# Loads of the first batch and the last two groups in a top-k attention + highway kernel

## The chip, the cores and the metric

One core of one Trainium2 chip. The time is the device time of the kernel in microseconds; the kernel before was run three times and the median is given. Beside it stands one profiled execution, whose span runs from its first to its last instruction.

## What is computed

For 8 batches of 8 heads, with 576 rows of 64 numbers: scores are q·kᵀ/8; in each row of scores only the 32 largest are kept; softmax over these; the product with v. The heads are laid side by side into a matrix x of 4608 x 512, and a highway layer follows.

```python
scores = scale * np.matmul(q, k.transpose(0, 1, 3, 2))
kth = np.partition(scores, -top_k, axis=-1)[..., -top_k:-top_k + 1]
scores = np.where(scores >= kth, scores, -1000000000.0)
attn = np.exp(scores - max); attn = attn / (sum + 1e-09)
x = heads_side_by_side(np.matmul(attn, v))
H = np.maximum(x @ w_h, 0.0)
T = 1.0 / (1.0 + np.exp(-(x @ w_t + b_t)))
out = T * H + (1.0 - T) * x
```

## The kernel before

**Units.** The rows of a batch are taken as five query tiles: four of 128 rows and a rest of 64 rows, in which two heads share the 128 partitions. A *group* is a query tile with all 8 heads of a batch; the two rests of two neighbouring batches are joined into one highway group. Inside a group the work goes in *pairs* of tiles (two tiles of 128 x 576 scores), and two pairs are a *quad*. `n` counts the pairs, 144 in all. `step` runs over them, and each step works on several pairs at different stages.

**A pair.** `scores` (L190) makes 8 matmuls into `ps`, a PSUM tile of four banks of which there is one (`bigps`). `evac` (L210): ScalarE writes relu(scores) to a buffer `z`. `tree` (L221): VectorE takes the maximum of the two halves of each row into `hi`; this reads `ps`, and frees it. For a quad `folds` (L236) halves twice more (`hh`, `h3`) and puts minima into the list buffer `w2`. `minima` (L251): GpSimd forms the matching minima of `hh` and `hi` by integer arithmetic, in four instructions. `tops` and `rest` (L272, L293) are VectorE's lists: MAX8 and MATCH_REPLACE8 on these short rows until the 32nd largest of each row stands in `m4`. `mask` (L368): ScalarE makes a penalty `pen` from z and that threshold. `trans` (L411): TensorE transposes z and adds the penalty into PSUM, 4 chunks per tile into `zt` (two buffers) and the last chunk of both tiles into `zr` (one buffer); ScalarE takes exp of each into `et`. `av` (L444): product with v into the rest of `zr`; ScalarE copies it to `xs`.

**A group.** `norm` (L478) divides by the sums, which gives `g.x`. The highway layer is `ffn_x` (transposes of x to `xT`, and half of x as `xh`), `ffn_h` (x·w_h), `ffn_r`/`ffn_d` (relu, minus xh), `ffn_t` (x·w_t, Tanh), `ffn_e` and `ffn_o` (products and sum, and the DMA of the result). Its PSUM comes from `ffn_bank` (L492).

**Order.** Nearly all instructions of TensorE, VectorE, ScalarE and GpSimd go through `Pinned` (L25): they keep the order in which the program writes them on their engine. So the profile gives L35, the line of that helper, for nearly all of them, and tiles tell them apart. DMAs by `nc.sync` (the SP queue) and by the plain `nc.scalar` are not pinned; a scheduler places them.

**The start.** `early` (L726) prepares the first batch: for each of four head pairs `prep_pair` (L130) loads k and q (each as two halves of 128 KB and a rest of 32 KB), transposes them by TensorE (`kqps`), and copies them to `kT` and `qT`, q by VectorE. Load buffers are in pairs (`ldpool`, 2). For pair 0 the second halves of k and q go by ScalarE's queue, unpinned; all others by SP. 24 warm-up transposes of the identity stand before the first real ones.

**The end.** From L855 the last three pairs (`m`, `m+1`, `m+2`) and the last two groups (`gp`, the second-last; `gl`, the last, `final`) are written out by hand. `judge_lists`, `judge_scales` and `judge` reduce flags over the whole run, which tell whether a slow exact loop has to be run after all (L893); it is not run with this data.

Of the kernel before, what the change touches and what calls it, by code (L numbers as in the profile page):

```python
# [8 lines left out]
AF = mybir.ActivationFunctionType  # L9
# [30 lines left out]
class PinnedCore:  # L40
    def __init__(self, tc):
        for name in ("tensor", "vector", "scalar", "gpsimd"):
            setattr(self, name, Pinned(tc, getattr(tc.nc, name)))
        self.sync = tc.nc.sync


class Group:
# [19 lines left out]
class Ops:  # L67


    def __init__(self, ctx, tc, shared, exact):  # L70
        self.tc = tc
        self.nc = tc.nc if exact else PinnedCore(tc)
        self.__dict__.update(shared)
        self.exact = exact
        s = "g" if exact else ""

        def pool(name, bufs, **kw):
            return ctx.enter_context(tc.tile_pool(name=name + s, bufs=bufs, **kw))

        PS = bass.MemoryType.PSUM  # L80
        self.ldpool = pool("ld", 2)
        self.kqpool = pool("kq", 1 if exact else 2)
        self.scpool = pool("sc", 2) if exact else None
        self.treepool = pool("tree", 3)
        self.wpool = pool("w", 4)
        self.lpool = pool("l", 2)
        self.etpool = pool("et", 2)
        self.xpool = pool("x", 2)
        self.fpool = pool("f", 2)
        self.bigps = pool("bigps", 1, space=PS)  # L90
        self.ztps = pool("ztps", 2, space=PS)
        self.zrps = pool("zrps", 1, space=PS)
        self.fps = pool("fps", 1, space=PS)
        self.st = {}
        self.quads = {}

    def load_pair(self, src, hp, name, eng=None, other=None):
        nc, D, S, R, P = self.nc, self.D, self.S, self.R, self.P  # L100
        JP = J * P
        eng = eng or nc.sync
        if name == "vin":
            t = self.ldpool.tile([P, 2, J + 1, D], FP32, tag=name, name=name)
            eng.dma_start(
                t[:, :, 0:J, :].rearrange("p h j d -> p h (j d)"),
                src(hp, 0, JP).rearrange("h (p j) d -> p h (j d)", j=J),
            )
            eng.dma_start(t[0:R, :, J, :], src(hp, JP, S).rearrange("h p d -> p h d"))
            return t  # L110
        t = self.ldpool.tile([P, J + 1, 2, D], FP32, tag=name, name=name)
        for hh in range(2):
            (other if other and hh else eng).dma_start(
                t[:, 0:J, hh, :],
                src(hp, 0, JP)[hh].rearrange("(p j) d -> p j d", j=J),
            )
        rest = lambda: eng.dma_start(
            t[0:R, J, :, :], src(hp, JP, S).rearrange("h p d -> p h d")
        )
        if other:  # L120
            return t, rest
        rest()
        return t
# [6 lines left out]
    def prep_pair(self, srcs, hp, prep, qeng=None, early=False):  # L130
# [2 lines left out]
        JP = J * P  # L133
        kT, qT, vb = prep
        ins = {}

        def load():
            if qeng:
                ins["k"], k_rest = self.load_pair(srcs[1], hp, "kin", None, qeng)
                ins["q"], q_rest = self.load_pair(srcs[0], hp, "qin", None, qeng)  # L140
                k_rest()
                q_rest()
            else:
                ins["k"] = self.load_pair(srcs[1], hp, "kin")
                ins["q"] = self.load_pair(srcs[0], hp, "qin")
            if not early:
                load_v()

        def load_v():
            ins["v"] = self.load_pair(srcs[2], hp, "vin")  # L150

        def main(name, dst):
            if early:
                kqps = self.ztps.tile([P, 512], FP32, tag="zt", name="kqps")
            else:
                kqps = self.fps.tile([P, 512], FP32, tag="fp", name="kqps")
            for c in range(J):
                nc.tensor.transpose(
                    kqps[:, c * P : (c + 1) * P],
                    ins[name][:, c, :, :].rearrange("p h d -> p (h d)"),  # L160
                    self.ident[:],
                )
            if early and name == "q":
                nc.vector.tensor_copy(dst[:, hp, 0:JP], kqps[:])
            else:
                nc.scalar.copy(dst[:, hp, 0:JP], kqps[:])
# [69 lines left out]
    def folds(self, k, g, pi):  # L236
# [4 lines left out]
        if pi == 0:  # L241
# [2 lines left out]
        vec.tensor_tensor(hh[:], hi[:, :, 0:H2], hi[:, :, H2:H1], ALU.max)  # L244
        a, b = hh[:, :, 0:H3], hh[:, :, H3:H2]
        vec.tensor_tensor(h3[:], a, b, ALU.max)
        return vec.tensor_tensor(
            g.w2[:, 2 * pi : 2 * pi + 4, H3:H2], a, b, ALU.min
        )

    def minima(self, k, after):  # L251

# [3 lines left out]
        hi, hh, h3 = self.quads[k]  # L256
        z = self.zbufs[k % NZ]
        sci, hii, hhi = [a[:].bitcast(I32) for a in (z, hi, hh)]
        head = gp.tensor_tensor(hhi, hii[:, :, 0:H2], hhi, ALU.subtract)
        self.tc.add_manual_dep(  # L260
            head.ins,
            after.ins.name,
# [2 lines left out]
            ),  # L265
            reason="after the folds",
        )
        gp.tensor_tensor(hhi, hhi, hii[:, :, H2:H1], ALU.add)
        gp.tensor_tensor(hii, sci[:, :, 0:H1], hii, ALU.subtract)
        gp.tensor_tensor(hii, hii, sci[:, :, H1:S], ALU.add)  # L270

    def tops(self, g, t, h3, hl):  # L272
# [135 lines left out]
                dst, pen[:, ti, cs], self.nident[:], start=False, stop=True  # L408
            )

    def trans(self, n, final=False):  # L411
        nc, P = self.nc, self.P
        JP = J * P
        z, pen = self.st[n].pop("z"), self.st[n].pop("pen")
        et = self.etpool.tile([P, 2, J + 1, P], BF16, tag="et", name="et")

        def ends():
            zr = self.zrps.tile([P, 512], FP32, tag="zr", name="zr")
            for ti in range(2):
                self.chunk_T(zr[:, ti * P : (ti + 1) * P], z, pen, ti, J)  # L420
            nc.scalar.activation(
# [4 lines left out]
            )  # L426
            self.st[n].update(et=et, zr=zr)

        if not final:
            ends()  # L430
        for ti in range(2):
            zt = self.ztps.tile([P, JP], FP32, tag="zt", name="zt")
            for c in range(J):
                self.chunk_T(zt[:, c * P : (c + 1) * P], z, pen, ti, c)
# [3 lines left out]
                AF.Exp,  # L438
                scale=self.scale,
            )  # L440
        if final:
            ends()

    def av(self, n, g, pi, vb):  # L444
        nc, P = self.nc, self.P
# [32 lines left out]
    def norm(self, g):  # L478
# [3 lines left out]
        rinv = self.scales[:, g.gi, :]  # L482
        nc.vector.reciprocal(rinv[0:ql, :], xs3[:, :, D])
        g.x = self.xpool.tile([P, H * D], FP32, tag="x", name="x")
        (nc.vector if g.final else nc.gpsimd).tensor_tensor(
            g.x[0:ql, :].rearrange("p (h d) -> p h d", h=H),
            xs3[:, :, 0:D],
            rinv[0:ql, :].unsqueeze(2).to_broadcast([ql, H, D]),
            ALU.mult,
        )  # L490

    def ffn_bank(self, g, name, other=False):  # L492
        if g.final or other:
            return self.ztps.tile([self.P, 512], FP32, tag="zt", name=name)
        return self.fps.tile([self.P, 512], FP32, tag="fp", name=name)
# [87 lines left out]
    def ffn_o(self, g, *dsts):  # L583
        ql = g.rows
        o = self.fpool.tile([self.P, self.dm], FP32, tag="o", name="o")
        eng = self.nc.vector if g.final else self.nc.gpsimd
        eng.tensor_tensor(o[0:ql, :], g.x[0:ql, :], g.d[0:ql, :], ALU.add)
        n = ql // len(dsts)
        for i, dst in enumerate(dsts):
            self.nc.sync.dma_start(dst, o[i * n : (i + 1) * n, :])  # L590
# [3 lines left out]
def kernel(  # L594
# [65 lines left out]
    with ExitStack() as cm:  # L660
# [62 lines left out]
        def have(n):  # L723
            return 0 <= n < NPR

        early = [  # L726
            prep(0, hp, nc.scalar if hp == 0 else None, True) for hp in range(NHP)
        ]
        early[0][0]()
        early[1][0]()  # L730
        warm = ops.fps.tile([P, 512], FP32, tag="fp", name="warm")
        for _ in range(24):
            ops.nc.tensor.transpose(warm[:, 0:P], ident[:], ident[:])
        for piece in early[0][1:4]:
            piece()
        ops.scores(0, *pairs[0], preps[0])
        ops.evac(0)
        ffn = []
# [16 lines left out]
            vec.tensor_reduce(bad[:, 3:4], bad[:, 0:3], op=ALU.max, axis=AX.X)  # L755

        def judge():
            bps = ops.fps.tile([P, 512], FP32, tag="fp", name="bps")
            ops.nc.tensor.transpose(bps[0:1, 0:P], bad[:, 3:4], ident[:])
            vec.tensor_reduce(flag_f[:], bps[0:1, 0:P], op=ALU.max, axis=AX.X)  # L760
            vec.tensor_copy(flag[:], flag_f[:])
# [11 lines left out]
        while step <= NPR:  # L773
            n = step
            if have(n):
# [3 lines left out]
                if n + 1 < NHP:  # L779
                    for piece in early[n + 1][1:4]:  # L780
                        piece()
                    if n + 2 < NHP:
                        early[n + 2][0]()
                    else:
                        for e in early[0:2]:
                            e[5]()
            if n == 5:
                load_weights()
# [24 lines left out]
            if NHP - 1 <= n < 2 * NHP - 1:  # L813
                e = n + 1 - NHP
                early[e][4]()
                if e + 2 < NHP:
                    early[e + 2][5]()
            ended = False
            if have(n - 5):
                g, pi = pairs[n - 5]  # L820
# [1 line left out]
            if n % 2:  # L822
                gens = ops.lists_rest(n // 2 - 1, *pairs[n - 3]) if have(n - 3) else []
                late = gens[2:]
                gens = gens[0:2]
                ops.run(gens)
                if kind == "t":
                    ops.ffn_e(fg)
# [1 line left out]
                ops.run(late, 2)  # L830
            else:
                ops.run(late)
                gens = ops.lists(n - 2, *pairs[n - 2]) if have(n - 2) else []
                ops.run(gens, 2)
                if kind == "h":
                    ops.ffn_d(fg)
                if ended:
# [26 lines left out]
        ops.ffn_e(fg)  # L864
        ops.ffn_o(fg, *out_rows(fg))
        ops.run(late)
        values(m)
        ops.trans(m + 1)
        ops.norm(gp)
        ops.settle(gl)  # L870
        ops.mask(m + 2, *pairs[m + 2])
        ops.ffn_x(gp)
        values(m + 1)
        ops.trans(m + 2, final=True)
        ops.ffn_h(gp)
        ops.ffn_r(gp)
        ops.ffn_d(gp)
        values(m + 2)
        ops.norm(gl)
        ops.ffn_t(gp)  # L880
        ops.ffn_x(gl)
        ops.ffn_e(gp)
        ops.ffn_o(gp, *out_rows(gp))
        judge_lists()
        judge_scales()
        ops.ffn_h(gl)
        ops.ffn_r(gl)
        ops.ffn_d(gl, ops.ffn_t(gl))
        judge()
        ops.ffn_e(gl)  # L890
        ops.ffn_o(gl, *out_rows(gl))

    taken = nc.values_load(flag[0:1, 0:1], min_val=0, max_val=1)  # L893
    with tc.If(taken > 0):
# [64 lines left out]
```

## Time and profile before

| what | us |
|---|---|
| median of three runs | 888.23 (886.67 to 888.36) |
| the profiled execution | 888.35 |
| its span | 886.6 |
| first scores start on TensorE | 8.41 |
| VectorE's last list ends | 863.6 |
| VectorE's last instruction ends | 879.36 |
| mean granted TensorE clock | 0.95 |

A view by stretches gives VectorE 0.03 us of work in the first 7.6 us, 5.40 in the next 13.4, 814.18 in the 819 us from 21 to 840, 23.13 in the 23.6 to 863.6, and 8.61 in the last 15.8 before 879.4. In timeline lines the first column is the start in us from the span's start, the second the time from the first start to the last end of the merged instructions, then engine (ACTq, SPq: the queue that issues a DMA), line, operation, tile written <- tiles read, shapes, count, and in brackets the idle time before it and what ended it. In lines of waits, the numbers are us in total, times, and the longest.

### The profile page before, as it was taken

To read this page: it belongs to the slowest core of one execution; us is meant where nothing else is said; L and a number is where in the kernel's file an instruction comes from. 1 tells how busy PE (TensorE), PEld (TensorE's weight loads), DVE (VectorE), ACT (ScalarE), POOL (GpSimd) and SP (SyncE) were. 2 spreads that over 40 slices of the span, in tenths; PEclk is the share of its full clock that TensorE was granted. 3 is DMA by queue.
4 is the path that set the end of the run, shared out by engine and by line. 5 is a ranking of instruction groups with operands and counts; after the bars stand their busy time and mean duration, and the time that the engine had idled before them with its cause. 6 is when DMAs were issued, how large, how long until landed. Compare 5 with 4: busy or idle time off the path is not lost.

```text
span 886.6 us, 20024 instructions
## 1 busy us (share of the span) xinstructions
PE 712.9 (80%) x6573; PEld 503.8 (57%) x6573; DVE 851.3 (96%) x4198; ACT 700.7 (79%) x1333; POOL 724.8 (82%) x452
## 2 busy tenths in 40 slices
PE   6678978878877888788788797887988789877874
PEld 5456655655555565565565565665555556555553
DVE  2999999999999999999999999999999999999993
ACT  3688878888788887888788887888978888777762
POOL 5788888888878889888887888878887888888872
PEclk9799999999999999999999999999999999898888
DMA  6362110322012220212202211032201300000001
GB/s 150 78 115 74 44 36 13 81 54 53 14 39 67 54 53 13 54 41 53 54 13 65 60 45 42 14 81 65 53 14 28 80 13 14 13 13 1 14 25 28
DMA packets 96671, 40.29 MB, mean 45 GB/s; under 512 B 82608, under 2 KB 91952, under 8 KB 96560
## 3 DMA queue, kind: packets, MB, share of 16 engines
q1 hardware_dynamic: 94304, 37.51, 16.5%
q0 software_dynamic: 1200, 1.18, 0.8%
q8 instruction: 53, 0.87, 0.4%
q14 instruction: 58, 0.48, 0.2%
q10 hardware_dynamic: 1056, 0.26, 0.1%
HBM read 30.67 MB, written 9.44 MB: 45 GB/s over the span
## 4 chain that ended last, share of the span: by engine, by line
DVE 86%; PE 6%; ACT 5%; issue 1%; POOL 0%; ACTq 0%; POOLq 0%
DVE w L35 45%; DVE m L35 17%; DVE hi L35 10%; DVE hh L35 6%; DVE h L35 3%; PE ps L35 3%; DVE d L35 3%; ACT z L35 2%; ACT et L35 2%; PE zt L35 1%; ACT pen L35 1%; PE zr L35 1%; PE tps L35 1%; PE warm L35 1%; DVE scales L35 0%
## 5 line engine op out<-in xcount | busy, mean ns | idle before, releaser
L35 PE MATMUL ps<-kT,qT 64*128 64x64 f32 (+3 forms) x1280 | 215.4, 462 | 91.1 <-DVE hi L35 86.5
L35 ACT ACTIVATE z<-ps 128x1152 f32<-128x1152 f32 x144 | 163.2, 1133 | 111.0 <-PE ps L35 109.5
L35 ACT ACTIVATE pen<-z,m 128x576 bf16<-128x576 f32 x288 | 225.9, 786 | 0.1
L35 PE MATMUL zt<-ident,z 128*128 128x128 f32 x1152 | 225.5, 289 | 0.3
L35 PEld LDWEIGHTS ps<-kT,qT 64*128 64x128 f32 (+1 forms) x1280 | 108.2, 184 | 191.2 <-DVE hi L35 95.8
L35 PE MATMUL zt<-nident,pen 128*128 128x128 bf16 x1152 | 214.7, 225 | 0.0
L35 POOL TENSOR_TENSOR hh<-hi,hh 128x576 int32<-128x576 int32 x72 | 101.7, 1413 | 124.3 <-DVE w L35 124.3
L35 POOL TENSOR_TENSOR hi<-hi,z 128x1152 int32<-128x1152 int32 x72 | 190.3, 2642 | 5.6
L35 POOL TENSOR_TENSOR hi<-z,hi 128x1152 int32<-128x1152 int32 x72 | 189.3, 2629 | 5.6
L35 PEld LDWEIGHTS zt<-ident,z 128*128 128x128 f32 x1152 | 169.7, 147 | 19.3 <-ACT xT L35 1.0
L35 ACT ACTIVATE et<-zt 128x512 bf16<-128x512 f32 x288 | 161.6, 606 | 13.5 <-PE zt L35 12.6
L35 PEld LDWEIGHTS <-pen 128*128 128x128 bf16 x1440 | 160.0, 111 | 1.5 <-ACT pen L35 1.3
L35 DVE MAX8 m<-w 128x8 f32<-128x168 f32 x576 | 160.3, 320 | 0.0
L35 DVE MAX8 w<-hi 128x8 f32<-128x288 f32 x288 | 116.7, 447 | 0.1
L35 DVE TENSOR_TENSOR hi<-ps,z 128x576 f32<-128x576 f32 x144 | 106.5, 740 | 8.2 <-ACT z L35 8.2
L35 POOL TENSOR_TENSOR hh<-hh,hi 128x576 int32<-128x576 int32 x72 | 101.3, 1407 | 5.6
L35 PE MATMUL zr<-v,et 128*128 128x65 bf16 (+1 forms) x1600 | 89.6, 196 | 15.9 <-ACT et L35 13.0
L35 PEld LDWEIGHTS <-et 128*128 128x128 bf16 (+1 forms) x1600 | 70.3, 101 | 52.6 <-ACT et L35 36.5
L35 DVE MATCH_REPLACE8 w<-m,w 128x168 f32<-128x168 f32 x288 | 89.3, 318 | 0.0
L35 DVE MAX8 w<-hh 128x8 f32<-128x72 f32 x576 | 84.1, 219 | 0.0
L35 PE MATMUL zr<-ident,z 128*128 128x128 f32 x288 | 74.9, 314 | 3.6 <-ACT xs L35 3.5
L35 DVE TENSOR_TENSOR hh<-hi 128x576 f32<-128x576 f32 x72 | 62.2, 865 | 2.5
(71 smaller groups left out, 1153.9 us busy)
## 6 DMA issues: line engine op xcount, KB each, us to landing
vin<-in_v_dram SPq DMA_DIRECT2D x32, 256.0 KB, 3.0
out_dram<-o SPq DMA_DIRECT2D x32, 256.0 KB, 2.3
kin<-in_k_dram SPq DMA_DIRECT2D x63, 128.0 KB, 3.0
qin<-in_q_dram SPq DMA_DIRECT2D x63, 128.0 KB, 2.9
kin<-in_k_dram SPq DMA_DIRECT2D x32, 32.0 KB, 2.5
qin<-in_q_dram SPq DMA_DIRECT2D x32, 32.0 KB, 2.5
vin<-in_v_dram SPq DMA_DIRECT2D x32, 32.0 KB, 2.6
out_dram<-o SPq DMA_DIRECT2D x8, 128.0 KB, 2.4
```

The source lines that it names most:

```text
L35: return self._tc.keep_in_program_order(fn(*args, **kw))
```

## The change

At the start: the loads of the first batch are pinned to their queues (a new `queue` wraps `nc.sync`, and `ops.nc.scalar` takes the place of `nc.scalar`); there are three load buffers, so the loads of three head pairs are written first; the second halves of k and q go by ScalarE's queue for head pairs 0 and 1; v follows behind the loads of the fourth pair. The 24 warm-ups become 12 before k's transposes and 3 before q's. The q copies of head pairs 2 and 3 go to ScalarE. For the first quad VectorE makes the minimum of `hh` itself, so that GpSimd has two instructions there, not four, and the first two rounds of its lists are written into step 1.

```diff
-        self.ldpool = pool("ld", 2)
+        self.ldpool = pool("ld", 2 if exact else 3)
...
+        eng = nc.queue if early else nc.sync
...
-            if qeng:
-                ins["k"], k_rest = self.load_pair(srcs[1], hp, "kin", None, qeng)
-                ins["q"], q_rest = self.load_pair(srcs[0], hp, "qin", None, qeng)
+            if early:
+                ins["k"], k_rest = self.load_pair(
+                    srcs[1], hp, "kin", eng, qeng, True
+                )
+                ins["q"], q_rest = self.load_pair(
+                    srcs[0], hp, "qin", eng, qeng, True
+                )
                 k_rest()
                 q_rest()
...
-            if early and name == "q":
+            if early and name == "q" and hp < 2:
                 nc.vector.tensor_copy(dst[:, hp, 0:JP], kqps[:])
...
+        if k == 0:
+            last = vec.tensor_tensor(
+                hh[:], hi[:, :, 0:H2], hi[:, :, H2:H1], ALU.min
+            )
+        return last
...
-        early[0][0]()
-        early[1][0]()
+        for e in early[0:3]:
+            e[0]()
...
-        for _ in range(24):
-            ops.nc.tensor.transpose(warm[:, 0:P], ident[:], ident[:])
-        for piece in early[0][1:4]:
-            piece()
+        spin(12)
+        early[0][1]()
+        spin(3)
+        early[0][2]()
+        early[0][3]()
...
+                if n == 1:
+                    opening = ops.lists(0, *pairs[0])
+                    ops.run(opening, 2)
```

At the end: `trans` is split into `parts`, so that the transposes, exps and penalties of the last pairs can be written in another order. The four banks of `ps`, no longer needed for scores, are handed out: three to the second-last group's highway layer, the fourth to the last pair in place of `zr`, and two of the first again to the last group's Tanh product. The last group's x, xT and final product are done in halves of 256 columns, each half of the result leaving on SP's and ScalarE's queues at once (64 rows each). The flag reductions move to earlier places on VectorE, and `norm` of the second-last group moves from GpSimd to VectorE.

```diff
+    def final_t(self, g, banks):
+        nc, n_g = self.nc, self.n_g
+        W = self.dm // 2
+        g.tp = [b[:, 0:W] for b in banks]
+        for j, tp in enumerate(g.tp):
+            cs = slice(j * W, (j + 1) * W)
+            for i in range(n_g):
+                nc.tensor.matmul(
+                    tp, g.xT[:, i, :], self.wt[:, i, cs],
+                    start=(i == 0), stop=False,
+                )
+            nc.tensor.matmul(
+                tp, self.cst[:], self.bt[:, cs], start=False, stop=True
+            )
+            nc.scalar.activation(tp, tp, AF.Tanh)
+    def final_o(self, g, dsts, queues):
+        vec, P = self.nc.vector, self.P
+        W = self.dm // 2
+        n = P // len(dsts)
+        o = self.fpool.tile([P, self.dm], FP32, tag="o", name="o")
+        for j, tp in enumerate(g.tp):
+            cs = slice(j * W, (j + 1) * W)
+            vec.scalar_tensor_tensor(
+                out=g.d[:, cs], in0=tp, scalar=1.0, in1=g.d[:, cs],
+                op0=ALU.add, op1=ALU.mult,
+            )
+            vec.tensor_tensor(o[:, cs], g.x[:, cs], g.d[:, cs], ALU.add)
+            for i, dst in enumerate(dsts):
+                queues[i].dma_start(dst[:, cs], o[i * n : (i + 1) * n, cs])
...
     def ffn_bank(self, g, name, other=False):
+        if g.last and not g.final:
+            return self.spare.pop(0)
...
         values(m)
-        ops.trans(m + 1)
+        part, ends = ops.parts(m + 1)
+        part(0)
+        ops.mask(m + 2, *pairs[m + 2], tis=(0,))
+        part(1)
+        ops.mask(m + 2, *pairs[m + 2], tis=(1,))
+        ends()
         ops.norm(gp)
         ops.settle(gl)
-        ops.mask(m + 2, *pairs[m + 2])
-        ops.ffn_x(gp)
+        part, ends = ops.parts(m + 2, banks[3])
+        ends()
+        part(0)
         values(m + 1)
-        ops.trans(m + 2, final=True)
-        ops.ffn_h(gp)
-        ops.ffn_r(gp)
-        ops.ffn_d(gp)
+        ops.ffn_x(gp)
+        part(1)
+        judge_lists()
         values(m + 2)
         ops.norm(gl)
-        ops.ffn_t(gp)
-        ops.ffn_x(gl)
+        ops.ffn_h(gp)
+        ops.ffn_r(gp)
+        ops.final_x(gl)
+        ops.ffn_d(gp)
+        ops.ffn_t(gp)
+        judge_scales()
         ops.ffn_e(gp)
         ops.ffn_o(gp, *out_rows(gp))
-        judge_lists()
-        judge_scales()
         ops.ffn_h(gl)
         ops.ffn_r(gl)
-        ops.ffn_d(gl, ops.ffn_t(gl))
+        ops.ffn_d(gl)
         judge()
-        ops.ffn_e(gl)
-        ops.ffn_o(gl, *out_rows(gl))
+        ops.final_t(gl, banks[0:2])
+        ops.final_o(gl, out_rows(gl), (nc.sync, ops.nc.scalar))
```

`final_x` takes the four 128-wide chunks of x in two halves: two transposes each into a `zt` bank, the first half to `xT` by VectorE, the second by ScalarE, which then makes `xh`.

## The prediction

> **What bounds the kernel now.** I read the page's busy shares first, then VectorE's (DVE's) waits, then the two ends of the run in the timeline, since a chain of waits that is 86% VectorE leaves only the ends open.
>
> ```profile
> PE 712.9 (80%) x6573; PEld 503.8 (57%) x6573; DVE 851.3 (96%) x4198; ACT 700.7 (79%) x1333; POOL 724.8 (82%) x452
> DVE 86%; PE 6%; ACT 5%; issue 1%; POOL 0%; ACTq 0%; POOLq 0%
> DVE hi L35 <- ACT z L35: 8.2, 4, 2.6
> DVE qT L35 <- PE kqps L35: 7.6, 1, 7.6
> DVE xT L35 <- PE xtps L35: 3.0, 2, 2.2
> DVE d L35 <- PE hps L35: 2.9, 1, 2.9
> ```
>
> VectorE is busy 851.3 of 886.6 us. Its idle 35.3 us lies at the start (7.6 us until the first transposed q, then three waits of 2.64 us for a z before `hi`), at the end (3.0 + 2.9 + 1.0 us before its last instruction), and in 7.2 us from that instruction's end, 879.36, to the end of the span. In between it is full, so what the change can win is there. Two places need the clock times.
>
> ```profile
> 0.74 0.66 ACTq L113 DMA_DIRECT2D kin<-in_k_dram  x1
> 2.10 1.28 ACT L626 ACT_TABLE_LOAD   x1 [2.10 <-issue]
> 5.05 0.63 SPq L117 DMA_DIRECT2D kin<-in_k_dram  x1
> 1.58 5.09 PE L35 MATMUL warm<-ident 128*128 128x128 f32 x24 [1.58 <-POOL ident masks.py:199]
> 6.50 0.60 PE L35 MATMUL kqps<-ident,kin 128*128 128x128 f32 x4
> 8.41 1.30 PE L35 MATMUL ps<-kT,qT 64*128 64x512 f32 x8 [0.61 <-DVE qT L35]
> 12.41 1.30 PE L35 MATMUL ps<-kT,qT 64*128 64x512 f32 x8 [1.41 <-DVE qT L35]
> 26.41 2.14 PE L35 MATMUL ps<-kT,qT 64*128 64x512 f32 x8 [3.04 <-DVE hi L35]
> 20.56 0.76 DVE L35 TENSOR_TENSOR hi<-ps,z 128x576 f32<-128x576 f32 x1 [2.64 <-ACT z L35]
> 876.08 0.58 ACT L35 ACTIVATE tps<-tps 128x512 f32<-128x512 f32 x1 [3.19 <-PE tps L35]
> 877.97 0.67 DVE L35 SCALAR_TENSOR_TENSOR d<-tps,d 128x512 f32<-128x512 f32 x1
> 878.67 0.69 DVE L35 TENSOR_TENSOR o<-x,d 128x512 f32<-128x512 f32 x1
> 879.39 2.15 SPq L590 DMA_DIRECT2D out_dram<-o  x2
> ```
>
> ScalarE (ACT) issues its two loads at 0.74, ahead of its table load. By the issue-to-landing times they are in at 3.4 and 5.4, all of pair 0's six loads by 6.1; so the first transposes (6.50) wait for the 24 warm-up matmuls alone, and the first scores start at 8.41.
>
> **Start, loads.** The changed program, as built, has on ACT's queue: table load, `nident`, and then the four pinned loads. They use the completion counters again that the eight SP loads ahead of them took: the second half of pair 0's k waits until SP's seventh load (pair 1's k rest) has landed, the second half of its q until SP's eighth has; pair 1's two wait for SP's ninth and tenth. Queued behind them on ACT are the kT copies, which wait for these data anyway; SP's pair-3 loads also wait for ACT's first. SP issues one load per 0.67 us (2.38, 3.08, 3.73, 5.05), so the seventh goes at 0.75 + 6*0.67 = 4.77. A 32 KB rest there takes 2.5 us: 7.27. ACT then issues k at 7.3; a 128 KB half takes 2.7 (ACT, 0.74) to 3.3 us (SP, 0.75): in at 10.0 to 10.6, I take 10.3. The q half follows at 8.0 and takes 2.7 to 4.1 us (the 1.43 and 1.51 issues: 4.0, 4.1): 10.7 to 12.1, I take 11.4. PE: four k transposes from 10.35 at 0.21 us (24 in 5.09), three spins 0.64, to 11.83; q 0.85 + 0.2 to drain; DVE's qT copy 0.70; issue 0.14: first scores at 13.75, not 8.41: **+5.3 us** (best +3.8, with PE at full clock and q in at 10.7; worst +5.8).
>
> **Start, clock.** Twelve warm-ups end near 4.1 and PE is idle for 6 us. After 3.0 us idle, in the row at 26.41, the eight score matmuls take 2.14 us and the next 2.40, at a granted clock of 0.50, against 1.30 at 8.41; that half clock held from 26.7 to 36.95. So the first two scores cost +0.9 each: **+1.8** (0 to 1.8, and up to 1.1 more if the fourth is slow too: then `hi` waits 1.3 us instead of 0.2).
>
> The Trainium skill ("TensorE: Matmul & The Clock Gate", Part 1) says that about 3.4 us of sustained work brings the full clock back, where this trace took 10.2 us with gaps; by it only the first scores would be slow, and the sum would be 0.9 lower.
>
> **Start, what it gains.** Counted from the end of the second scores, E1 (13.72 before). Before: `hi` ends E1+1.96, folds 1.55, DVE copies qT, scores at E1+4.35, next `hi` at E1+6.84 (20.56). After: ACT copies kT and qT (2*0.59) behind z's 1.14, so scores can start at E1+2.5 and z is out at E1+5.0; DVE meanwhile does folds 1.55, the added min over 576 (0.77, price of the row hh<-hi), four MAX8 (0.54) and four MATCH_REPLACE8 (0.80), and is at the next `hi` at E1+5.64: 1.2 earlier, with no gap. After it DVE is spared a qT copy 0.60 and the 1.34 done already; it waits 0.2 for the fourth `hi`. Gain 1.2 + 1.94 - 0.2 = **-2.95 us** (-1.8 with a slow clock). GpSimd's first minima drop from four to two (8.2 to 5.3 us), due only 7 us after the folds end; that side is free. The third buffer lets pair 2 load without waiting for a free one: nothing, pair 2's transposes start after 20. v's loads move behind pair 3's on SP and land near 20; they are used after the fifth z: nothing.
> Start: 5.3 + 1.8 - 2.95 = **+4.15** (low +0.9: best arrival 3.8, full clock; high +5.8 + 1.8 - 1.8 = +5.8).
>
> **Middle.** Same instructions, DVE full: 0.
>
> **End.** Up to DVE's last list (863.6) all is as before. Then, on the clock of before: ACT's pens and exps alternate, the last pen 866.55 (before 868.1): 1.5 earlier. From there PE's ends 0.3, zt 0.7, av 0.8, x transposes 0.45, zt 0.7, exp 0.6, av 0.5, copy 0.4 bring the last values to 870.97 (before 871.36), but DVE is in the list check (1.88 from 869.45): reciprocal 871.37 (before 871.39). x in two halves (0.34 apart, from the 288- and 512-wide rows) 872.36.
> The spare banks are four slices of one tile, and the built program orders them as one: the second-last group's t product waits for its `d`, the final t's first half for its `ffn_e`, the second half for the first half's Tanh, and DVE's first half for the second Tanh. So: xT half 872.8, `d` 873.5, t product 1.24 to 874.8, Tanh 0.58, `ffn_e` to 876.1; first half on PE 0.65 and Tanh 0.37 to 877.2, second half 0.7 + 0.37 to 878.35; then `d`, `o`, `d`, `o` of 256: out at 879.22 and 880.0. Before: 879.36. DVE's last product is 0.6 later; but its two DMAs leave on two queues at 880.0, where the second of before left at 879.97 and landed 3.5 us on. 64 KB instead of 128 KB takes 2.3 (the smallest out row) to 3.5 us, I take 3.1: **-0.4** (-1.2 at 2.3; +1.0 if PE falls to half clock there, which doubles the 1.24 and part of the 0.65). The flag load, ahead of SP's part and not of ACT's, hid in 1.4 us before and has 2.2 now.
>
> **Sum.** 4.15 - 0.4 = +3.75 on the profiled 888.35 (span 886.6): 892.1. The median is 888.23, 0.12 below, within the runs' own spread. What a measurement can tell from no change is 0.2%, 1.8 us: slower means over 890.0, faster under 886.45.
>
> **Rivals.**
> (A, forecast, 0.58) ACT's late halves decide: 890.3 to 893.8, **892.1**.
> (B, 0.18) The late halves land early. Place: the q half. At its low bound with full clock it costs +0.9 at the start, and with -1.2 at the end 888.05; with -0.4, 888.85. For: landings of 2.7 us in the rows. Against: SP is issuing beside it, as at 1.5, where it took 4.0. Not slower than before once q is in by 10.3 at full clock: then first scores 1.44 later (0.6 + 0.70 + 0.14), 11.74, a delay of 3.35 that 2.95 and 0.4 pay back.
> (C, 0.17) The end turns worse as well: one tile for four banks, PE at half clock in its gaps, +1.0, with the start at +5.8: 895.2. For: clock 0.50 from 859.56 to 862.97. Against: it was 1.00 from 863 to 880.
> (D, 0.07) It does what its words say: loads in by 6, first scores as before, so -2.95, and banks without the shared waits: second half on PE right behind the first, 1.3 earlier, t product not behind `d`, 0.7, and the 0.4: 883.0. For: the 2.64 us gaps. Against: the waits in the built program.
>
> Faster is D, 0.07; within 0.2% B less what ends above 890.0, 0.16; slower the rest, 0.77. The range runs from B's low end, 0.25 off for the spread of runs, to C's: 887.8 to 895.2, and leaves out D.
>
> **What would show it.** ACT's four load issues at 7.3 to 9.7, not near 2.4; first transposes at 10.0 to 10.6 and first scores near 13.7; score groups of 2.1 us at first; `hi` gap of 2.64 gone after the second; second Tanh half ending before DVE's first. Wrong if ACT issues its loads by 3 us, or the second-last pen ends later than 866 relative to the lists.

## The result, and the profile after

The changed kernel takes 892.36 us (median of four runs, 892.03 to 893.84), the kernel before 888.30 beside it (four runs, 886.67 to 889.84): 1.0049 times as long, 95% interval 1.0028 to 1.007. That is +4.1 us where +3.75 was forecast. The profiled page comes from another execution, with a span of 889.1 us against 886.6. That is +2.5: the page lies below all four timed runs of the changed kernel, whose spans are 890.3 to 892.1, so its parts add up to less than the +4.1 of the medians.

The page's busy line and its chain:

```profile
PE 707.5 (80%) x6527; PEld 500.9 (56%) x6569; DVE 851.5 (96%) x4201; ACT 701.5 (79%) x1338; POOL 719.5 (81%) x448
...
DVE 89%; PE 4%; ACT 4%; POOL 1%; issue 1%; DMA 1%; SPq 0%; ACTq 0%; POOLq 0%; DVEq 0%
```

VectorE works as long as before (851.5 us, 851.3 before); what changed is how long it stands still. Its two waits at the start:

```profile
DVE qT L35 <- PE kqps L35: 13.6, 1, 13.6
DVE hi L35 <- ACT z L35: 6.6, 3, 3.7
```

The first wait has grown from 7.6 to 13.6 us and the `hi` waits have shrunk from 8.2 to 6.6: less than the first one cost. The timeline of the changed kernel's start shows why:

```profile
0.74 1.28 ACT L707 ACT_TABLE_LOAD   x1 [0.74 <-PEq L1049]
2.04 0.31 ACT L707 ACTIVATE nident<-ident 128x128 bf16<-128x128 f32 x1
4.82 0.63 SPq L35 DMA_DIRECT2D kin<-in_k_dram  x1
7.29 0.67 ACTq L35 DMA_DIRECT2D kin<-in_k_dram  x1
8.00 0.64 ACTq L35 DMA_DIRECT2D qin<-in_q_dram  x1
10.67 1.09 PE L35 MATMUL kqps<-ident,kin 128*128 128x128 f32 x4 [6.28 <-DMA kin<-in_k_dram]
12.43 1.09 PE L35 MATMUL kqps<-ident,qin 128*128 128x128 f32 x4
14.40 2.40 PE L35 MATMUL ps<-kT,qT 64*128 64x512 f32 x8 [0.47 <-ACT qT L35]
19.56 1.30 PE L35 MATMUL ps<-kT,qT 64*128 64x512 f32 x8 [0.50 <-ACT qT L35]
26.53 0.75 DVE L35 TENSOR_TENSOR hi<-ps,z 128x576 f32<-128x576 f32 x1
29.92 0.76 DVE L35 TENSOR_TENSOR hi<-ps,z 128x576 f32<-128x576 f32 x1 [0.21 <-ACT z L35]
```

ScalarE is free at 2.35 and issues nothing until 7.29, when SP's seventh load (issued at 4.82) has had 2.5 us to land. TensorE idles 6.28 us for that data. The first scores start at 14.40 instead of 8.41. The gain is there too: the third `hi`, which waited 2.64 us before, starts with no wait.

At the end, in the changed kernel's timeline:

```profile
879.97 0.37 ACT L35 ACTIVATE ps<-ps 128x256 f32<-128x256 f32 x1 [1.52 <-DVE flag_f L35]
880.39 0.60 PE L35 MATMUL ps<-wt,xT 128*128 128x256 bf16 x4 [0.46 <-ACT ps L35]
881.20 0.37 ACT L35 ACTIVATE ps<-ps 128x256 f32<-128x256 f32 x1 [0.85 <-PE ps L35]
881.60 0.42 DVE L35 SCALAR_TENSOR_TENSOR d<-ps,d 128x256 f32<-128x256 f32 x1 [1.46 <-ACT ps L35]
882.50 1.36 SPq L570 DMA_DIRECT2D out_dram<-o  x2
882.85 0.42 DVE L35 TENSOR_TENSOR o<-x,d 128x256 f32<-128x256 f32 x1
```

The second half's product (880.39) waits for the first half's Tanh, and VectorE's first `d` (881.60) for the second half's Tanh, though each half has a bank to itself.

Five marks of the profiled executions carry the comparison: start of the first scores, first MAX8 on `hi` (from there on VectorE is full), end of the last list, end of VectorE's last product, end of the span.

| kernel | first scores | first MAX8 of hi | lists end | last product ends | span |
|---|---|---|---|---|---|
| before | 8.41 | 27.92 | 863.6 | 879.36 | 886.6 |
| after | 14.40 | 32.24 | 867.5 | 883.27 | 889.1 |
| start only | 14.13 | 33.10 | 869.3 | 886.3 | 893.4 |
| end only | 9.03 | 29.79 | 865.1 | 881.65 | 887.6 |
| loads first | 7.16 | 23.84 | 860.1 | 875.85 | 881.6 |
| banks apart | 14.58 | 32.90 | 868.5 | 883.07 | 890.3 |
| more warm-up | 13.65 | 32.61 | 868.0 | 885.09 | 891.0 |
| loads first, without the list order | 7.82 | 26.49 | 861.9 | 878.83 | 884.8 |
| loads first, q copies on VectorE | 7.45 | 28.18 | 863.6 | 879.36 | 885.1 |
| both | 7.84 | 26.30 | 861.7 | 875.51 | 882.8 |
| three queues | 7.87 | 24.55 | 860.3 | 873.82 | 880.4 |
| first half by ScalarE | 8.04 | 25.54 | 860.75 | 873.90 | 879.9 |
| loads first, again | 7.43 | 25.14 | 860.9 | 876.62 | 882.5 |

Between the pages of before and after, the first MAX8 is 4.3 later, lists to last product the same 15.8, last product to the span's end 5.8 instead of 7.2.

Each row is one execution, and the marks move from one to the next where the code is the same. With the old start (before, end only) the first MAX8 stands at 27.92 and 29.79, with the changed one (after, start only, banks apart) between 32.24 and 33.10, with the loads first in the changed start (four kernels, five pages) between 23.84 and 26.30. The stretch from the lists' end to the last product takes 15.8 to 17.0 us with the old end and 15.7 to 17.1 with the new one while its four banks are one tile; it is over 16.5 on the three pages of the new end where TensorE had a granted clock of 0.50 in the last 5 us ahead of the lists' end (end only, more warm-up, without the list order), and 15.7 or 15.8 on the four that had not (after, loads first in both its rows, q copies on VectorE).

### The profile page after: what moved, and what is told of

The parts are those of the page before. It is cut to its first block, busy times and chain, and to the rows that moved or that the text cites. A ratio compares the mean times of both kernels' runs of the same rounds, so it can differ in the third digit from the quotient of the medians.

```text
span 889.1 us, 19981 instructions
## 1 busy us (share of the span) xinstructions
PE 707.5 (80%) x6527; PEld 500.9 (56%) x6569; DVE 851.5 (96%) x4201; ACT 701.5 (79%) x1338; POOL 719.5 (81%) x448
## 4 chain that ended last, share of the span: by engine, by line
DVE 89%; PE 4%; ACT 4%; POOL 1%; issue 1%; DMA 1%; SPq 0%; ACTq 0%; POOLq 0%; DVEq 0%
DVE w L35 47%; DVE m L35 18%; DVE hi L35 10%; DVE hh L35 7%; DVE h L35 3%; DVE d L35 3%; PE ps L35 3%; ACT z L35 2%; ACT et L35 1%; DMA kin<-in_k_dram 1%; POOL hi L35 1%; PE kqps L35 1%; PE tps L35 1%; SPq L35 0%; DVE scales L35 0%
```

## The experiments

**The halves of the change, each alone.** The first kernel has the new start and the old end, the second the old start and the new end.

> The start of the changed kernel with the end of the old one. Theory (the late second halves of k and q on ScalarE's queue cost more than the rearranged lists win): the whole loss is here. ScalarE's four loads are issued at 7.3 to 10 us, first scores near 14.4, VectorE's first MAX8 of hi near 32.2 (27.9 before), its last list about 4 us later than before's 863.6, time near 892.5, slower by 4 to 5 us. Rival (the loss is shared by the end): slower by 2 us or less, and the new end slower by as much when it runs alone.

> The end of the changed kernel with the start of the old one. Theory: VectorE's last list ends near 863.6 as before, its last instruction 15.8 us later as in both profiles, and the two half DMAs on two queues shorten what follows from 7.2 to 5.8 us: 1.4 us faster, 887, not to be told from no change by the time alone. Rival (the end costs): 1 us or more slower.

Start only: 892.61 us (890.69 to 895.15), 1.0045 times before, 1.0028 to 1.0062. End only: 887.54 (886.54 to 889.32), 0.9992, 0.9982 to 1.0002. The whole loss is in the start; the end can't be told from no change. On its page the lists end 1.5 us later than on that of before, where the same mark had been expected: TensorE had a granted clock of 0.50 from 17.8 to 38.2, and the third and fourth scores took 2.40 us each.

**ScalarE's loads ahead of its table load.** In the start, only the place of one line is changed: `nident`, whose activation brings the table load with it, is written behind the loads, and pinned like them.

```diff
-    nc.scalar.mul(nident[:], ident[:], -STEEP)
...
         for e in early[0:3]:
             e[0]()
+        ops.nc.scalar.mul(nident[:], ident[:], -STEEP)
```

> The changed kernel with the write of nident, and so ScalarE's table load, behind its four loads. Theory (in the program as built, the table load in front lets SP's eight loads take the eight completion counters first, and ScalarE's loads wait for those to land): ScalarE issues at 0.74 to 3 us, first scores at 8.2 to 9, first MAX8 of hi near 25 (32.2 in the changed kernel, 27.9 before), 7 us faster than the changed kernel and 4 faster than before: near 884. Rival (the loads are late for the traffic of six loads and of SP's queue, not for the counters): first scores still after 11 us, time above 888.

It takes 883.68 us (883.4 to 884.92), 0.9956 of before, 0.9939 to 0.9973. The waits of the two built programs (the counters of completed DMAs are DMAHW0 to 7) differ in this:

```
changed kernel, ScalarE:  table load; nident; kin [waits DMAHW6]; qin [waits DMAHW7]; kin [DMAHW0]; qin [DMAHW1]
loads first, ScalarE:     kin; qin; kin; qin; table load; nident
loads first, SP:          kin; qin; kin; qin; kin [waits DMAHW0]; qin [DMAHW1]; kin [DMAHW2]; qin [DMAHW3]
```

Eight counters go round over the loads of both queues in the scheduler's order. Behind the table load, ScalarE's loads came fifteenth to eighteenth, after fourteen of SP's; now they are among the first eight, and SP's fifth is the first that waits. In the timeline of this kernel:

```profile
0.74 0.67 ACTq L35 DMA_DIRECT2D kin<-in_k_dram  x1
...
3.48 1.28 ACT L35 ACT_TABLE_LOAD   x1 [3.48 <-issue]
...
7.16 1.29 PE L35 MATMUL ps<-kT,qT 64*128 64x512 f32 x8
...
18.12 0.74 DVE L35 TENSOR_TENSOR hi<-ps,z 128x576 f32<-128x576 f32 x1
```

First scores at 7.16, the third `hi` again without a wait, the first MAX8 of `hi` 8.4 us earlier than in the changed kernel. So the late issue is the loss, and what the start does beside it gains.

**Four tiles for the four banks**, in the changed kernel, with the order of work unchanged:

```diff
-        big = ops.bigps.tile([P, 2, 1024], FP32, tag="big", name="ps")
+        ops.bigcm.close()
+        bankps = cm.enter_context(
+            tc.tile_pool(name="bankps", bufs=1, space=bass.MemoryType.PSUM)
+        )
         banks = [
-            big[:, i // 2, i % 2 * 512 : (i % 2 + 1) * 512] for i in range(4)
+            bankps.tile([P, 512], FP32, tag=f"bank{i}", name=f"bank{i}")
+            for i in range(4)
         ]
```

> The changed kernel with four PSUM tiles of one bank each at the end, in place of four slices of one tile; the order of instructions is the same. Theory (waits between instructions on different slices hold up the end): t product of the second-last group no longer behind d, second half's product right behind the first's, first half's VectorE work not behind the second Tanh; from VectorE's last list to its last instruction 13.8 us in place of 15.8, 2 us off the changed kernel's time: near 890.4. Rival (VectorE's own order sets the end): less than 0.5 us.

It takes 890.15 us (889.21 to 892.1), 1.002 of before, 1.0008 to 1.0031; 2.2 us below the changed kernel. ScalarE's two half Tanhs in its timeline:

```profile
880.75 0.37 ACT L35 ACTIVATE bank<-bank 128x256 f32<-128x256 f32 x1 [0.94 <-PE bank L35]
881.29 0.37 ACT L35 ACTIVATE bank<-bank 128x256 f32<-128x256 f32 x1 [0.18 <-PE bank L35]
```

They stand 0.54 apart instead of 1.23, and VectorE takes its first half while the second is made. From the lists' end to the last product it is 14.6 us instead of 15.8, where 13.8 was expected; from the start of the second-last group's `xT` on VectorE, 9.0 instead of 11.5. That last stretch does not depend on the execution: it is 11.5 on all seven pages of kernels with the new end and one tile, 9.0 on all four with separate tiles. The expectation had not foreseen that the last product is now 1.4 us further from the span's end (7.2) than in the changed kernel; the kernel with both gains, below, shows why.

**More warm-up.** `spin(12)` becomes `spin(52)` in the changed kernel.

> The changed kernel with 52 warm-up transposes instead of 12 ahead of k's, so that TensorE is busy until shortly before k's half lands (near 10). Theory (the start lost its time to two things, the late loads and the clock that fell while TensorE stood idle): k's four transposes take 0.66 instead of 1.09, the first scores 1.30 instead of 2.40, and start at 13.9 instead of 14.40; they end 1.6 earlier, and the first MAX8 of hi stands near 30.6 instead of 32.24; time 890.0 to 891.2. Rival (the late data alone): scores end at most 0.3 earlier, time 892 to 893.

It takes 892.52 us (891.5 to 893.11), 1.0046 of before, 1.0031 to 1.0062: no better than the changed kernel, and not for the rival's reason. k's transposes ran at full speed (0.63) and the first scores started at 13.65, but took 2.40 all the same, and so did the second. The view by stretches (start and end, length, TensorE's busy time and matmuls, its granted clock, DMA share, GB/s) has, here,

```profile
14.00:16.00 2.00, 2.00 (x9) 0.50 0.54 122
```

and in the changed kernel:

```profile
14.00:16.00 2.00, 1.60 (x4) 1.00 0.29 65
```

Both kernels ran the first scores at half speed, one with a granted clock of 0.50 and one with 1.00, so a granted clock of 1.00 in the record doesn't say that TensorE ran at full speed. In the changed kernel the first spell of 0.50 began at about 29.2, here at about 13.2. That the 40 extra matmuls brought it forward is not shown: the page of the first half by ScalarE, with 12 warm-ups, has such a spell from 8.5 to 11.8. What the half speed costs this start was not won back by this edit.

**Without the first quad's new list order**, on the kernel with the loads first: no minimum by VectorE (GpSimd forms all four again), no two list rounds ahead of the third `hi`.

```diff
-        if k == 0:
-            last = vec.tensor_tensor(
-                hh[:], hi[:, :, 0:H2], hi[:, :, H2:H1], ALU.min
-            )
...
-                if n == 1:
-                    opening = ops.lists(0, *pairs[0])
-                    ops.run(opening, 2)
```

> The kernel with the loads first, but without the first quad's minimum by VectorE and without the two list rounds ahead of the third hi: the order of before in these places. Theory (as in the prediction's sum: with the q copy on ScalarE the third hi can start 0.7 earlier than where the opening puts it, so the 1.34 of list work and the 0.77 of the minimum fill a gap of some 1.3 and the fourth hi waits in their place): the lists end 0.5 to 1.0 later than with them, time near 884.4, hi waits 2.0 in the third place. Rival (the filled gap of the kernel before, 2.64, is the gain): lists end 2 to 2.6 later, time 886.

It takes 885.9 us (884.55 to 886.55), 0.9968 of before, 0.9954 to 0.9982: 2.2 above the kernel with the loads first, as much as the rival had said, by a way that neither had. The fourth `hi` ends as long after the second scores as with the lists (9.88 us, 9.82 with them), as the theory had it. Then:

```profile
22.47 2.62 POOL L35 TENSOR_TENSOR hi<-hi,z 128x1152 int32<-128x1152 int32 x1
23.04 2.68 DVE L35 TENSOR_TENSOR hh<-hi 128x576 f32<-128x576 f32 x1
```

VectorE's next fold takes 2.68 us instead of 0.76 and ends 0.63 behind GpSimd's instruction. With four minima GpSimd is still at work when the fold comes; with two, in the kernel with the loads first, it has ended at 22.33, as the fold begins. By these rows the minimum on VectorE pays by keeping the two apart; no run has the minimum without the list rounds.

It is no single case. In the kernel before, 51 of the 72 folds `hh<-hi` start while a GpSimd instruction is running, and each of them ends 0.61 to 0.63 us behind the end of that instruction, however long that has still to run (the folds take 0.81 to 1.52 us); the other 21 take 0.76.

The Trainium skill ("SBUF — State Buffer", section "SBUF: two separate sides") says that VectorE, in an instruction with two SBUF inputs, and GpSimd hold a shared pair of ports in turn, each for a whole instruction. The 2.68 here agrees, and so do the 51 folds of the kernel before.

**The q copies of head pairs 2 and 3 back on VectorE**, again on the kernel with the loads first:

```diff
-            if early and name == "q" and hp < 2:
+            if early and name == "q":
```

> The kernel with the loads first, but with the q copies of head pairs 2 and 3 back on VectorE, where they stand behind the work that now fills the gap. Theory (ScalarE's copies are what lets the third scores start at E1+2.2 instead of E1+4.35): third scores start 1.5 to 2.5 later, the third hi waits again for z by 1 to 2 us, and with the two copies of 0.68 back on VectorE the lists end 2 to 3 us later; time 885.7 to 886.7. Rival (the copies are hidden on either engine): lists end at most 1.4 later, the price of the copies alone; time 884 to 885.

It takes 887.68 us (886.09 to 889.66), 0.9999 of before, 0.9984 to 1.0014: 4.0 above the kernel with the loads first, where the theory said 2 to 3. The third scores:

```profile
17.89 1.59 PE L35 MATMUL ps<-kT,qT 64*128 64x512 f32 x8 [3.86 <-DVE m L35]
```

They start 5.15 us behind the second ones' end, 2.18 with ScalarE's copy: 3.0 later, where 1.5 to 2.5 had been expected. The copy for them, at 17.06, stands behind VectorE's folds and the minimum that now follows them, and ends at 17.75. So with this order the copy belongs on ScalarE; what the copies on VectorE cost without it was not run.

**Both gains together**: loads first and banks apart.

> Made of the two runs that gained: the changed kernel with ScalarE's table load and nident behind its four loads, and with four tiles of one bank each for the spare banks at the end. Theory (the two gains lie in different places, start and tail, and VectorE is full between them, so they add): the time of the kernel with the loads first, 883.7, less the 1.5 to 2.5 us that the banks apart gave: 881.2 to 882.2, ratio to before 0.992 to 0.994; in the profile first scores near 7.2, and from VectorE's end of the lists to its last product's end 14.6 instead of 15.8. Rival (the tail of the separate banks only looked shorter because TensorE's clock stood otherwise there): 883 to 884, the tail 15.3 or more.

It takes 883.82 us (882.81 to 884.64), 0.9947 of before, 0.9933 to 0.996: no better than the loads alone (883.68), where 881.2 to 882.2 was expected. Two things stand against the gain on these pages. The start is behind: the first MAX8 stands at 26.30 instead of 23.84 with the same start code, since TensorE's half speed covered the first scores (2.40 us instead of 1.29) and part of the fourth (1.96). And at the end, from the lists' end to the last product it is 13.8 us, even less than expected, but from there to the span's end 7.3 instead of 5.75. The timeline of its last two microseconds of work, and below it the read of the flag by SP (its length in ns as least, median and most; its start):

```profile
874.30 0.43 DVE L35 TENSOR_TENSOR o<-x,d 128x256 f32<-128x256 f32 x1
874.76 1.34 ACTq L35 DMA_DIRECT2D out_dram<-o  x2
875.09 0.42 DVE L35 TENSOR_TENSOR o<-x,d 128x256 f32<-128x256 f32 x1
875.70 2.08 SPq L575 DMA_DIRECT2D out_dram<-o  x2
```

```profile
L1008 SPq TENSOR_LOAD <-flag x1: 525/525/525, 874.7 to 874.7; - x1
```

The first half is ready at 874.73. ScalarE issues its part at once. SP has just begun its read of the flag and issues 0.94 behind ScalarE, the second half at 876.3, 0.8 behind the last product, taking 1.5 us to issue. The page of the banks apart alone has the same: half ready at 882.29, read from 882.3, issue at 883.25. In the changed kernel SP's read began at 880.9 and SP stood waiting for the half at 881.8, 0.6 before it was ready.

**The first half by another queue**, to take SP's flag out of the way: in the kernel with both, SP issues only its part of the second half.

```diff
-                queues[i].dma_start(dst[:, cs], o[i * n : (i + 1) * n, cs])
+                queues[j][i].dma_start(dst[:, cs], o[i * n : (i + 1) * n, cs])
...
-        ops.final_o(gl, out_rows(gl), (nc.sync, ops.nc.scalar))
+        ops.final_o(gl, out_rows(gl), ((ops.nc.gpsimd, ops.nc.scalar), (nc.sync, ops.nc.scalar)))
```

The second kernel has `ops.nc.scalar` where this has `ops.nc.gpsimd`; the third is the one with the loads first again, beside them.

> The kernel with both gains (loads first, banks apart), but the last group's first half of 256 columns leaves by GpSimd's and ScalarE's queues instead of SP's and ScalarE's; the second half by SP's and ScalarE's as before. Theory (in the run with both, SP still read the flag, from 874.7 to 875.7, when the first half was ready at 874.73, so that its two DMAs went 1.0 and 0.8 late, the second taking 1.5 to issue, and the 2 us won on VectorE were given back): SP's one DMA issues 0.2 behind VectorE's last instruction instead of 0.8, and the span ends 6.0 to 6.4 after that instruction's end instead of 7.3; time 882.5 to 883.2 beside 883.8, if GpSimd's own DMA lands within 4 us. Rival (the end of the span does not hang on SP's issue, or GpSimd's DMA is slower than SP's was): 7.3 or more, 883.8 to 885.

> As the run before, but both row halves of the first 256 columns leave by ScalarE's queue, which then issues three DMAs. Theory (issue on SP behind its read of the flag is what is late): SP's DMA as in the run before, ScalarE's third 0.6 behind the last product instead of at it; span's end 6.4 to 7.0 after VectorE's last instruction, time 883.0 to 883.6. Rival (the flag's read is not what holds the end): 7.3, 883.8.

> The kernel with the loads first alone, once more, beside these two on one chip, since it and the kernel with both came out alike (883.68 and 883.82) on two occasions. Theory (the banks apart win 2 us on VectorE and lose 1.5 at SP's late DMAs; first scores at half or full clock move the start by 1 to 2.5 us from run to run): 883.3 to 884.3, that is 0.3 to 1.5 above the three queues. Rival (the banks apart win nothing in the end, whatever the queues): the same time within 0.3 of the three queues.

Three queues: 881.59 us (881.39 to 883.42), 0.9928 of before, 0.9915 to 0.9941. First half by ScalarE: 881.81 (880.78 to 882.37), 0.9926, 0.9913 to 0.9939. Loads first alone: 884.87 (883.05 to 886.33), 0.9961, 0.9948 to 0.9974. The timeline of the three queues:

```profile
873.33 0.60 POOL L35 DMA_DIRECT2D out_dram<-o  x1 [0.70 <-DVE o L35]
873.40 0.42 DVE L35 TENSOR_TENSOR o<-x,d 128x256 f32<-128x256 f32 x1
873.99 0.47 SPq L575 DMA_DIRECT2D out_dram<-o  x1
```

SP's DMA now goes 0.17 behind the last product, and the span ends 6.6 us after that product (6.0 in the second kernel, 7.3 in the kernel with both), where 6.0 to 6.4 and 6.4 to 7.0 had been expected. So the rivals fall, and the banks apart with these queues stand 3 us below the loads alone, more than the 0.3 to 1.5 expected. These two kernels beat both the one before and the changed one. Their times are 0.9 and 1.2 us below the ranges expected. Part of their distance to the kernel with both lies ahead of the tail: on the pages their lists end 1.4 and 0.9 us earlier, and from there to the span's end it is 1.0 and 2.0 us less, of which 0.7 and 1.3 lie behind the last product. The kernel with both was not timed again beside them, and its interval (0.9933 to 0.996) overlaps theirs: the price of the queues alone is read from the pages.

## Why the prediction was right

The forecast, rival A, came in: late halves on ScalarE's queue decide the time. By its steps:

- **Loads, +5.3 us.** The issues came at 7.29 and 8.00, as worked out from SP's seventh and eighth loads. k's half landed in 3.2 us, at 10.5, and its data were used at 10.67 (10.35 predicted). q's half took 4.3 us, to 12.3, where 11.4, at most 12.1, had been taken, and q's transposes started at 12.43, 1.76 behind k's. Where q was in earlier (4.0 us on the page with the new start alone, 3.7 with the banks apart) they started 1.52 behind k's, as the 1.48 of the sum has it. So q's landing, on which rival B hung, cost about 0.25 us, and not in B's direction. First scores at 14.40, 0.65 later than predicted: +6.0, just past the worst case of +5.8.
- **Clock, +1.8 us.** +1.1 on this page: the first scores took 2.40, the second 1.30. The size was within the range, the row it came from was the wrong one. The 2.14 at 26.41 of before went with a granted clock of 0.50; here the record says 1.00 throughout, so what slows TensorE after an idle stretch does not show there. In the page with the new start alone both groups took 2.40, as forecast: by these rows the term is 1.1 in one execution and 2.2 in the other.
- The two errors cancel, and that is luck: the second scores end 7.15 us later than before, 7.1 predicted. On the page with the new start alone it is 8.0.
- **The start's gain, -2.95 us.** From the end of the second scores to the first MAX8 of `hi`: 14.21 before, 11.38 after, -2.83. The third `hi` started without a wait and the fourth waited 0.21, as said. Two of its reasons are priced by the runs, with the loads first: without the q copies on ScalarE the kernel is 4.0 us slower, more than the whole term, since the copy then stands behind the added minimum. And the sum called GpSimd's side "free" and gave fewer minima no price: with four of them, in the kernel without the new list order, VectorE's fold is held up 1.9 us.
- **Start, +4.15:** +4.32 at that MAX8, on these two pages. By the other pages with the same starts (27.92 and 29.79 before, 32.24 to 33.10 after) it lies between 2.5 and 5.2, so that it came this close is luck as well.
- **Middle, 0:** from there to the lists' end 835.7 before, 835.3 after.
- **End, -0.4 us.** VectorE's last product came 15.8 us after the lists' end, as before, where 0.6 more had been predicted; its output took 1.4 less to the span's end, where 1.0 was predicted. On the page -1.4; on the page with the new end alone it is 16.5 and 5.95, -0.5 together; by the ratio of that kernel's times 0.08%, -0.7 us, not told from zero. The waits between slices of one tile were as described, and four tiles took 2.5 us off. The flag's read on SP, named as hidden in 2.2 us, was hidden, and held up the output as soon as the tail was shorter.
- **The sum.** On the pages +4.32, -0.4 and -1.4 make +2.5; the medians say +4.1, and +3.75 was forecast. The mechanism is the one forecast; the nearness of the number rests on errors that cancel and on pages that differ by 1 to 2.5 us from execution to execution with the same code.

Rival D was what the change's words say: its 883.0 is close to what the kernel with the loads first reached, 883.68. The -2.95 and first scores 1.25 us earlier than before made that, without D's banks; with those and the flag out of the way it is 881.6.

Open: why TensorE's half speed at the start lasts so differently. In the kernel with both it held until 11.0, in the one with the loads first until about 4.8, with the same program ahead of it; on the five other pages with the loads first it ended between about 5 and 7.8.

## What to carry to other kernels

Pinning an order on each queue doesn't settle when a transfer starts: look in the built program at what each load waits for. Here eight completion counters were shared over the queues, and a load whose counter had been taken before waited for that earlier load to land. Slices of one tile were waited for as one tile, so banks that are to work independently need tiles of their own. A fold like VectorE's `hh`, with both inputs in SBUF, is best placed where no long GpSimd instruction runs. When a tail gets shorter, see what was hidden behind it: here SP's output DMAs, late behind its read of one flag, took back 1.5 of 1.9 us, and other queues for the first half gave 0.7 to 1.3 of it back.

## What the runs showed of the hardware

- TensorE ran at half speed in two ways: with a granted clock of 0.50, in spells of 3 (first half by ScalarE, 8.5 to 11.8) to 20 us (end only, 17.8 to 38.2), and with 1.00 granted, after idle time and in the first microseconds. When the first spell of 0.50 came differed between pages of the same start: 17.8 and 26.7 with the old one, 8.5 to 21.5 with the loads first.
- The Trainium skill ("TensorE: Matmul & The Clock Gate", Part 1) says that about 3.4 us of sustained work ends the slow state, by a window that runs freely. With the loads first, TensorE was at work from 1.58 and fast by about 4.8, which agrees; in the kernel with both it worked from 1.57 with gaps under 0.2 us and was slow until 11.0, which does not.
- With SP and ScalarE loading at once, ScalarE's 128 KB halves of k and q took 3.2 to 4.7 us to land in the changed kernel, and 2.7 and 4.0 before.
- A VectorE fold of 0.76 us that started while GpSimd was at work ended 0.61 to 0.63 us behind the end of GpSimd's instruction, 51 times of 51 in the kernel before; the longest, in the kernel without the list order, took 2.68.
